# A software pipeline and a flipped operand layout in the tap-generation stage of a long-convolution kernel

## Chip, cores, metric

One core of one Trainium2 chip. The metric is device time of one execution, in microseconds (us), lower is better. The kernel before took 1589.07 us (median of 12 runs, 1585.22 to 1591.90). All profiled runs of known state were fast.

The engines are called PE (TensorE matmuls), PEld (the weight loads of TensorE, which overlap PE), DVE (VectorE), ACT (ScalarE) and POOL (GpSimd), as in the profile.

## The reference, cut to what matters

The program is a state-space long convolution followed by a gated MLP. Only the first part is touched.

```python
def _A_ref(u, A_re, A_im, B_re, B_im, C_re, C_im, log_dt, Dskip):   # L = 2048, D = 576, N = 128
    ...
    P = jnp.exp(logdA[:, :, None] * l[None, None, :])               # (D, N, L)
    K = jnp.einsum('dn,dnl,dn->dl', Cc, P, dB).real                 # the taps, one filter per channel
    ...                                                             # FFT of taps and of u, product, inverse FFT
```

The kernel writes the position as `l = 64*l2 + l1` and splits the power: `K[d, l] = Re sum_n R[n, l1, d] * Q[n, l2, d]`. `R` (64 values of `l1`) is made with exp and sin, `Q` (32 values of `l2`) by repeated doubling (the "Q recurrence"), and the sum over the 128 states is a matmul of PE: 128 x 64 weights from `R`, a 128 x 32 moving operand from `Q`, two (real and imaginary) for each channel. The FFT is a matmul with slabs of cosines and sines.

## The kernel before

The stage works on two interleaved jobs. The first makes the taps, in 36 groups of 16 channels, two groups to a "pair", hence 18 pairs, 64 tap matmuls each. The second transforms the input `u` in 17 blocks of 64 matmuls (the last of 32); each block needs a fresh pair of slabs.

```python
    NCH = 16
    L1VX = Ar.alloc("l1vx", [128, NL1, NCH], BF16)          # 16 channels innermost
    ...
    RR = [Ar.alloc("rr%d" % i, [128, NL1, NCH], BF16) for i in range(2)]
    KST = [Ar.alloc("kst%d" % i, [NL1, NL2, 2 * NCH], BF16, ...) for i in range(2)]

    def r_args(sc):                                         # DVE: arguments of exp and sin
        pa_b = bass.AP(PAB, d0, [pst_of(PAB), [0, NL1], [1, NCH]])
        ...
        dve(lambda e: e.tensor_tensor(ARGA[k][:], L1VX[:], pa_b, ALU.mult), ...)
        dve(lambda e: e.tensor_tensor(ARGP[k][:], L1VX[:], pb_b, ALU.mult), ...)
    def r_acts(scs):                                        # ACT: exp for both groups, then sin
        ...
    def r_products(sc):                                     # DVE: RR = exp*cos, RI = exp*(-sin)
        ...
    def k_matmuls(sc):
        for sl in range(NCH):
            rq = bass.AP(QR, dq, [pst_of(QR), [DH, NL2]])
            lr = bass.AP(RR[c], sl, [pst_of(RR[c]), [NCH, NL1]])   # weights: one element every 32 bytes
            ...
            pe(lambda e: e.matmul(o_ap, lr, rq, start=True, stop=False), ...)
            pe(lambda e: e.matmul(o_ap, li, rqi, start=False, stop=True), ...)
        act(lambda e: e.activation(o_ap, i_ap, ACT.Copy), ...)     # eviction of the taps
        if c == 1:
            st(lambda e: e.dma_start(dst, KST[pr][:]), ...)        # store of the taps

    def gen_slab(dstc, dsts, kc, ks, block_b, nt):
        act(lambda e: e.activation(STMP[0][:, 0:nt, :], PSIS[:, 0:nt, :], ACT.Copy, scale=sphi), ...)
        act(lambda e: e.activation(STMP[1][:, 0:nt, :], PSIC[:, 0:nt, :], ACT.Copy, scale=sphi), ...)
        dve(lambda e: e.scalar_tensor_tensor(out=dstc..., in0=PSIC..., scalar=cphi, in1=STMP[0]...), ...)
        dve(lambda e: e.scalar_tensor_tensor(out=dsts..., in0=PSIS..., scalar=cphi, in1=STMP[1]...), ...)

    def do_pair(pair, nxt):
        ensure_args(pair); r_acts(pair)
        if nxt is not None: ensure_args(nxt)
        for sc in pair: r_products(sc)
        for sc in pair: k_matmuls(sc)
    ...                                                     # first Q recurrence, slabs and blocks mixed in
    for idx, pair in enumerate(pairs0):                     # nine rounds: taps, then a block
        do_pair(pair, nxt)
        slab_step()
        fwd_u_step()                                        # block: 64 matmuls, two evictions on ACT
    ...                                                     # second Q recurrence, slabs and blocks mixed in
    for idx, pair in enumerate(pairs1):                     # nine rounds, no block left
        do_pair(pair, nxt)
        fwd_u_step()
```

After the last round the taps are loaded again from memory in another arrangement (`b_kt<-scr_kd`), and PE transforms them. Everything from there on is the same code in both kernels.

Of the kernel before, what the change touches and what calls it, by code (L numbers as in the profile page):

```python
# [7 lines left out]
ALU = mybir.AluOpType  # L8
# [205 lines left out]
def build_kernel(nc, A_u, A_A_re, A_A_im, A_B_re, A_B_im, A_C_re, A_C_im,  # L214
# [252 lines left out]
    L1VX = Ar.alloc("l1vx", [128, NL1, NCH], BF16)  # L467
# [4 lines left out]
    act(lambda e: e.activation(L1VX[:], bass.AP(L1V, 0, [pst_of(L1V), [1, NL1], [0, NCH]]), ACT.Copy),  # L472
# [4 lines left out]
    ARGA = [Ar.alloc("arga%d" % i, [128, NL1, NCH], BF16) for i in range(NARG)]  # L477
    ARGP = [Ar.alloc("argp%d" % i, [128, NL1, NCH], BF16) for i in range(NARG)]
    ER = ARGA
    CR = [Ar.alloc("cr%d" % i, [128, NL1, NCH], BF16) for i in range(2)]  # L480
    SRN = ARGP
    RR = [Ar.alloc("rr%d" % i, [128, NL1, NCH], BF16) for i in range(2)]
    RI = [Ar.alloc("ri%d" % i, [128, NL1, NCH], BF16) for i in range(2)]
    KST = [Ar.alloc("kst%d" % i, [NL1, NL2, 2 * NCH], BF16, keys=["kst%d_0" % i, "kst%d_1" % i]) for i in range(2)]
    KBANKS = [4, 5, 6, 7]

    def r_args(sc):
        k = sc % NARG
        d0 = sc * NCH
        pa_b = bass.AP(PAB, d0, [pst_of(PAB), [0, NL1], [1, NCH]])  # L490
        pb_b = bass.AP(PBB, d0, [pst_of(PBB), [0, NL1], [1, NCH]])
# [21 lines left out]
    def k_matmuls(sc):  # L513
        c = sc % 2
        pr = (sc // 2) % 2
# [4 lines left out]
        for sl in range(NCH):  # L520
# [4 lines left out]
            lr = bass.AP(RR[c], sl, [pst_of(RR[c]), [NCH, NL1]])  # L525
            li = bass.AP(RI[c], sl, [pst_of(RI[c]), [NCH, NL1]])
# [7 lines left out]
        act(lambda e, o_ap=o_ap, i_ap=i_ap: e.activation(o_ap, i_ap, ACT.Copy),  # L534
            reads=[bkey], writes=["kst%d_%d" % (pr, c)])
        if c == 1:
            dst = bass.AP(Kd, d0 - NCH, [[D, NL1], [NL1 * D, NL2], [1, 2 * NCH]])
            st(lambda e, dst=dst, pr=pr: e.dma_start(dst, KST[pr][:]),
               reads=["kst%d_0" % pr, "kst%d_1" % pr], writes=["kd%d" % (sc // 2)])
# [9 lines left out]
    def gen_slab(dstc, dsts, kc, ks, block_b, nt):  # L549
        cphi = CPHI[:, block_b:block_b + 1]  # L550
        sphi = SPHI[:, block_b:block_b + 1]
        act(lambda e: e.activation(STMP[0][:, 0:nt, :], PSIS[:, 0:nt, :], ACT.Copy, scale=sphi),  # L552
            reads=["psis", "sphi"], writes=["stmp0"])
        act(lambda e: e.activation(STMP[1][:, 0:nt, :], PSIC[:, 0:nt, :], ACT.Copy, scale=sphi),  # L554
            reads=["psic", "sphi"], writes=["stmp1"])
# [27 lines left out]
    def fwd_block(i, srcbuf, srckey, is_k, BK=None, AK=None):  # L583
        r = i % NSLAB
        nyq = (i == NKB - 1)
        groups = [(0, 0), (0, 1)] if nyq else [(0, 0), (0, 1), (1, 0), (1, 1)]
        for (f, h) in groups:
# [15 lines left out]
            if h == 1:  # L603
                np_ = 1 if nyq else 128
                i_ap = bass.AP(PSALL, 2 * f * 512, [[PSPST[0], np_], [512, 2], [1, DH]])
                if not is_k:
# [3 lines left out]
                    act(lambda e, o_ap=o_ap, i_ap=i_ap: e.activation(o_ap, i_ap, ACT.Copy),  # L610
                        reads=[("fps", 2 * f), ("fps", 2 * f + 1)], writes=[dkey])
                else:
# [4 lines left out]
                    act(lambda e, o_ap=o_ap, i_ap=i_ap, sc_ap=sc_ap: e.activation(o_ap, i_ap, ACT.Copy, scale=sc_ap),  # L617
                        reads=[("fps", 2 * f), ("fps", 2 * f + 1), "scol"], writes=[dkey])
# [15 lines left out]

    first_half = list(range(NSC // 2))
    second_half = list(range(NSC // 2, NSC))
    pairs0 = [first_half[i:i + 2] for i in range(0, len(first_half), 2)]
    pairs1 = [second_half[i:i + 2] for i in range(0, len(second_half), 2)]
    fwd_done = [0]
    fwd_loaded = [0]  # L640
    slab_gen = [0]

    def slab_step():
        b = slab_gen[0]
        if b < NKB and b < fwd_done[0] + NSLAB:
            r = b % NSLAB
            gen_slab(SLC[r], SLS[r], "slc%d" % r, "sls%d" % r, b, T)
            slab_gen[0] += 1
# [536 lines left out]
```

## Time and profile before

| stretch of the kernel before (us) | what runs there |
|---|---|
| 62 to 130 | first Q recurrence on DVE, three blocks |
| 130 to 366 | nine rounds of one pair and one block |
| 366 to 434 | second Q recurrence on DVE, the remaining blocks |
| 434 to 578 | nine rounds of one pair alone |
| 578 to 591 | last store of taps and their reload |
| 591 to 1589 | rest of the program, code not touched |

The busy time by stretch of the kernel before comes first. The columns are the stretch with its length, the busy us (and instruction count) of PE, PEld, DVE, ACT and POOL, the granted clock of PE as a share of full speed, the share of the DMA engines and GB/s.

```profile
62.00:130.00 68.00, 28.04 (x192) 20.23 (x192) 56.24 (x59) 23.69 (x25) 0.00 (x0) 0.78 0.00 0
130.00:366.00 236.00, 165.11 (x1166) 136.53 (x1167) 87.97 (x90) 135.87 (x128) 9.84 (x9) 0.69 0.04 6
366.00:434.00 68.00, 37.55 (x276) 27.46 (x273) 56.50 (x59) 23.70 (x24) 0.00 (x0) 0.80 0.00 1
434.00:578.00 144.00, 72.82 (x576) 70.71 (x576) 46.19 (x72) 89.65 (x90) 8.72 (x8) 0.50 0.05 8
```

In the rounds no engine is full: from 130 to 366 us PE is busy 165 of 236 us, ACT 136, DVE 88. A stretch where nobody is full is bound by waits, and the list of waits of 62 to 590 us (engine and line, what it waited for, total us, times, longest) says which:

```profile
PE psall L527 <- DVE b_rr L510: 172.9, 18, 29.4
DVE b_rr L510 <- ACT b_cr L502: 145.5, 36, 12.2
DVE b_slc L556 <- ACT b_stmp L552: 113.8, 17, 9.4
ACT b_kst L534 <- PE psall L529: 105.8, 36, 3.3
```

PE waits for DVE's product, DVE for ACT's cosine, ACT for PE's taps: a circle. The timeline of one round shows it (start, length, engine, line, operation, in brackets the idle time before it and its releaser):

```profile
181.31 1.28 ACT L498 ACT_TABLE_LOAD   x1
182.61 2.00 ACT L498 ACTIVATE b_arga<-b_arga 128x1024 bf16<-128x1024 bf16 x2
...
187.10 0.69 DVE L510 TENSOR_TENSOR b_rr<-b_arga,b_cr 128x1024 bf16<-128x1024 bf16 x1 [7.17 <-ACT b_cr L502]
187.85 0.31 PE L527 MATMUL psall<-b_qr,b_rr 128*64 128x32 bf16 x1 [7.24 <-DVE b_rr L510]
...
196.78 0.59 ACT L534 ACTIVATE b_kst<-psall 64x512 bf16<-64x512 f32 x1 [3.30 <-PE psall L529]
```

ACT begins the exponentials at 181.31 only after it has evicted the block before (copied its result out of `psall`). PE idles 7.24 us until the product at 187.10 frees it, runs taps to 196.7, and then the block from 196.7 to 207.5; in the chain of waits the table load of the next exponentials follows at 208.15, so this round took 26.8 us. Nine rounds with a block take 236 us, nine without 144 us, 16 us each.

The groups of the two matmul operands that the layout touches (line, engine, operation, output<-inputs, shapes, count, busy us and mean ns of one, idle time before):

```profile
L527 PE MATMUL psall<-b_qr,b_rr 128*64 128x32 bf16 x576 | 140.9, 291 | 172.9 <-DVE b_rr L510 172.9
L527 PEld LDWEIGHTS psall<-b_qr,b_rr 128*64 128x64 bf16 x576 | 124.9, 217 | 176.9 <-DVE b_rr L510 176.9
L493 DVE TENSOR_TENSOR b_argp<-b_l1vx,b_pbb 128x1024 bf16<-128x1024 bf16 x36 | 24.7, 686 | 0.0
```

Matmuls overlap, so the 291 ns of one says little about the rate. What counts is the distance from one start to the next: inside a run of taps it is 0.12 us in the timeline, hence 7.7 us for the 64 taps of a pair. In this kernel all runs of taps fall in stretches with a granted clock of 0.50.

The stage ends with the reload of the taps. These lines of the chain of work that ended last (start, length, what) show PE resuming at 590.60 us, right on its landing:

```profile
578.01 3.85 DMA scr_kd<-b_kst
582.37 8.18 DMA b_kt<-scr_kd
590.60 109.44 PE psall L601 x875
```

### The profile page before, as it was taken

The numbers are of one execution on the slowest core, as the hardware profiler recorded it, in microseconds if no ns is written. First come the engines' busy times: TensorE is split into PE (matmuls) and PEld (weight loads), VectorE is DVE, ScalarE is ACT, GpSimd is POOL, SyncE is SP. The second block draws the span as 40 slices with busy tenths as digits, with TensorE's granted clock in tenths as the row PEclk, the third lists the DMA queues.
The fourth block names the chain that finished last, engine by engine and source line by source line (L and its number), as shares of the span: only waits on it lengthen the run. The fifth ranks groups of instructions, "written<-read, shape, count | busy, mean of one in ns | idle before, by whom it ended". The sixth has DMA issues, their size and how long they took to land.

```text
span 1588.8 us, 18520 instructions
## 1 busy us (share of the span) xinstructions
PE 1106.8 (70%) x7945; PEld 808.1 (51%) x7960; DVE 856.7 (54%) x1154; ACT 624.6 (39%) x600; POOL 61.7 (4%) x104
## 2 busy tenths in 40 slices
PE   0344767678255459991799718567866399999997
PEld 0223656566144447771577502122221388888886
DVE  8686343426942325558677607688666733333332
ACT  1524555554266646663254207676555100000000
POOL 0000000000000000000000100000000000000000
PEclk9976676769655559996899859695999699999999
DMA  4100000000000020000001151213432411111100
GB/s 108 41 1 4 4 7 4 7 7 1 1 7 10 8 74 1 1 1 0 22 32 38 74 124 53 70 32 93 113 96 60 138 44 44 44 44 44 44 9 8
DMA packets 92257, 60.15 MB, mean 38 GB/s; under 512 B 51280, under 2 KB 87504, under 8 KB 92176
## 3 DMA queue, kind: packets, MB, share of 16 engines
q1 hardware_dynamic: 86096, 38.52, 9.2%
q0 software_dynamic: 6080, 20.45, 3.9%
q8 instruction: 63, 1.03, 0.3%
q14 instruction: 18, 0.15, 0.0%
HBM read 26.61 MB, written 20.45 MB: 30 GB/s over the span
## 4 chain that ended last, share of the span: by engine, by line
PE 54%; DVE 23%; ACT 16%; DMA 4%; issue 2%; SPq 1%; POOL 0%; ACTq 0%; DVEq 0%; POOLq 0%
PE psall L1100 16%; PE psall L601 14%; PE psall L806 8%; PE psall L529 5%; DVE b_vb L886 4%; PE psall L527 4%; PE psall L1120 4%; ACT b_xsb L881 4%; PE psall L952 2%; DMA b_w2c<-in_B_w_in_dram 2%; ACT b_arga L498 2%; ACT b_x2b L883 2%; DVE b_x2b L885 1%; ACT L502 1%; DVE b_slc L556 1%
## 5 line engine op out<-in xcount | busy, mean ns | idle before, releaser
L1100 PE MATMUL psall<-b_wq,b_z 128*128 128x256 bf16 x2304 | 255.5, 274 | 28.8 <-DVE b_z L1051 28.8
L527 PE MATMUL psall<-b_qr,b_rr 128*64 128x32 bf16 x576 | 140.9, 291 | 172.9 <-DVE b_rr L510 172.9
L1100 PEld LDWEIGHTS psall<-b_wq,b_z 128*128 128x128 bf16 x2304 | 226.3, 98 | 57.1 <-issue 28.7
L556 DVE SCALAR_TENSOR_TENSOR b_slc<-b_psic,b_cphi,b_stmp 128x2048 bf16<-128x2048 bf16 (+1 forms) x50 | 119.0, 2379 | 180.1 <-ACT b_stmp L552 180.1
L527 PEld LDWEIGHTS psall<-b_qr,b_rr 128*64 128x64 bf16 x576 | 124.9, 217 | 176.9 <-DVE b_rr L510 176.9
L952 PE MATMUL psall<-b_w2c,b_hnt 128*128 128x512 bf16 (+3 forms) x393 | 111.6, 410 | 88.5 <-DMA b_w2c<-in_B_w_in_dram 59.6
L601 PE MATMUL psall<-b_xn,b_slc 128*128 128x288 bf16 (+1 forms) x544 | 96.1, 353 | 86.7 <-DVE b_slc L556 67.0
L529 PE MATMUL psall<-b_qi,b_ri 128*64 128x32 bf16 x576 | 140.0, 291 | 13.9 <-DVE b_ri L511 13.9
L806 PE MATMUL psall<-b_t,b_slc 128*128 128x288 bf16 x512 | 129.4, 290 | 27.3 <-DVE b_t L761 27.3
L1106 DVE TENSOR_TENSOR b_gt<-psall,b_bq 128x256 bf16<-128x256 f32 x144 | 61.1, 425 | 145.6 <-PE psall L1100 145.6
L806 PE MATMUL psall<-b_t,b_sls 128*128 128x288 bf16 x512 | 129.0, 289 | 14.7 <-DVE b_t L766 14.7
L552 ACT ACTIVATE b_stmp<-b_psis,b_sphi 128x2048 bf16<-128x2048 bf16 (+1 forms) x50 | 101.4, 2028 | 92.8 <-DVE b_slc L556 92.8
L881 ACT ACTIVATE b_xsb<-psall 128x1024 bf16<-128x1024 f32 (+1 forms) x84 | 75.7, 901 | 155.8 <-PE psall L952 63.3
L529 PEld LDWEIGHTS psall<-b_qi,b_ri 128*64 128x64 bf16 x576 | 124.9, 217 | 16.0 <-DVE b_ri L511 16.0
L886 DVE SCALAR_TENSOR_TENSOR b_vb<-b_x2b,b_xsb 128x1024 bf16<-128x1024 bf16 (+1 forms) x84 | 90.0, 1072 | 77.1 <-ACT b_x2b L883 75.9
L601 PEld LDWEIGHTS psall<-b_xn,b_slc 128*128 128x128 bf16 (+1 forms) x544 | 63.4, 119 | 116.4 <-DVE b_slc L556 66.9
L559 DVE SCALAR_TENSOR_TENSOR b_sls<-b_psis,b_cphi,b_stmp 128x2048 bf16<-128x2048 bf16 (+1 forms) x50 | 119.4, 2389 | 0.0
L952 PEld LDWEIGHTS psall<-b_w2c,b_hnt 128*128 128x128 bf16 (+1 forms) x400 | 35.5, 104 | 164.5 <-issue 129.4
L952 PE MATMUL psall<-b_hnt,b_w1c 128*128 128x512 bf16 (+1 forms) x352 | 95.1, 389 | 29.1 <-ACT b_xsb L881 26.3
L510 DVE TENSOR_TENSOR b_rr<-b_arga,b_cr 128x1024 bf16<-128x1024 bf16 x36 | 24.9, 692 | 145.5 <-ACT b_cr L502 145.5
L554 ACT ACTIVATE b_stmp<-b_psic,b_sphi 128x2048 bf16<-128x2048 bf16 (+1 forms) x50 | 101.4, 2027 | 5.1 <-DVE b_sls L559 5.1
L601 PE MATMUL psall<-b_kt,b_slc 128*128 128x288 bf16 (+1 forms) x544 | 72.6, 293 | 11.5 <-DMA b_kt<-scr_kd 11.5
(147 smaller groups left out, 1456.1 us busy)
## 6 DMA issues: line engine op xcount, KB each, us to landing
scr_wspt<-b_wst POOLq DMA_DIRECT2D x32, 256.0 KB, 2.3
b_wq<-scr_wspt SPq DMA_DIRECT2D x8, 1024.0 KB, 5.9
b_wout<-in_B_w_out_dram SPq DMA_DIRECT2D x1, 2592.0 KB, 9.3
scr_hnd<-b_hn POOLq DMA_DIRECT2D x4, 640.0 KB, 4.5
b_x<-in_A_u_dram SPq DMA_DIRECT2D x4, 576.0 KB, 5.8
scr_rd<-b_tmp POOLq DMA_DIRECT2D x2, 1152.0 KB, 6.5
scr_kd<-b_kst POOLq DMA_DIRECT2D x18, 128.0 KB, 3.8
b_kt<-scr_kd SPq DMA_DIRECT2D x2, 1152.0 KB, 6.9
```

The source lines that it names most:

```text
L527: pe(lambda e, o_ap=o_ap, lr=lr, rq=rq: e.matmul(o_ap, lr, rq, start=True, stop=False), reads=["rr%d" % c, "qr"], writes=([bkey] if sl == ...
L529: pe(lambda e, o_ap=o_ap, li=li, rqi=rqi: e.matmul(o_ap, li, rqi, start=False, stop=True), reads=["ri%d" % c, "qi"], writes=(), publish=(s ...
L552: act(lambda e: e.activation(STMP[0][:, 0:nt, :], PSIS[:, 0:nt, :], ACT.Copy, scale=sphi), reads=["psis", "sphi"], writes=["stmp0"])
L554: act(lambda e: e.activation(STMP[1][:, 0:nt, :], PSIC[:, 0:nt, :], ACT.Copy, scale=sphi), reads=["psic", "sphi"], writes=["stmp1"])
L556: dve(lambda e: e.scalar_tensor_tensor(out=dstc[:, 0:nt, :], in0=PSIC[:, 0:nt, :], scalar=cphi, in1=STMP[0][:, 0:nt, :], op0=ALU.mult, op1 ...
L559: dve(lambda e: e.scalar_tensor_tensor(out=dsts[:, 0:nt, :], in0=PSIS[:, 0:nt, :], scalar=cphi, in1=STMP[1][:, 0:nt, :], op0=ALU.mult, op1 ...
L601: pe(lambda e, o_ap=o_ap, lhsT=lhsT, rhs=rhs, j=j: e.matmul(o_ap, lhsT, rhs, start=(j == 0), stop=(j == T - 1)), reads=[skey, "%s%d" % (sr ...
L806: e.matmul(o_ap, slab[:, i, :], g[:, i, h * DH:(h + 1) * DH], start=first, stop=False),
L881: act(lambda e, xs=xs, ps=gc.ps_ap: e.activation(xs, ps, ACT.Copy), reads=gc.bkeys, writes=["xsb%d" % k])
L886: dve(lambda e, xs=xs, x2=x2, vb=vb: e.scalar_tensor_tensor(out=vb, in0=x2, scalar=GELU_C0, in1=xs, op0=ALU.add, op1=ALU.mult), reads=["xs ...
L952: pe(lambda e, o_ap=o_ap, lhsT=lhsT, rhs=rhs, g=g: e.matmul(o_ap, lhsT, rhs, start=(g == 0), stop=(g == NDT - 1)), reads=[lkeys[g]] + rkey ...
L1100: pe(lambda e, o_ap=o_ap, lhsT=lhsT, rhs=rhs, s_=s_: e.matmul(o_ap, lhsT, rhs, start=(s_ == 0), stop=(s_ == T - 1)), reads=["z2_%d" % s_, ...
```

## The change

Its intent is to break the circle: a block runs on PE while ACT and DVE prepare the next pair, the taps run one round late, their evictions later still, and the 17 blocks are spread over the rounds. Two more edits support this. The slab temporaries move from ACT to DVE for these blocks. And the layout of the `R` operands flips from channel-innermost to position-innermost, so the weights of a tap matmul become contiguous; in exchange, the argument products on DVE get an operand whose innermost step is 0 (one value read 64 times).

```diff
-    L1VX = Ar.alloc("l1vx", [128, NL1, NCH], BF16)
+    L1VX = Ar.alloc("l1vx", [128, NCH, NL1], BF16)
 ...                                     # the same for ARGA, ARGP, CR, RR, RI
+    NKST = 4                            # buffers for evicted taps, 2 before
 ...
-        pa_b = bass.AP(PAB, d0, [pst_of(PAB), [0, NL1], [1, NCH]])
+        pa_b = bass.AP(PAB, d0, [pst_of(PAB), [1, NCH], [0, NL1]])
 ...
-            lr = bass.AP(RR[c], sl, [pst_of(RR[c]), [NCH, NL1]])
+            lr = bass.AP(RR[c], sl * NL1, [pst_of(RR[c]), [1, NL1]])
 ...
+        if dve_only:                    # in gen_slab
+            dve(lambda e: e.tensor_scalar(STMP[0]..., PSIS..., sphi, None, op0=ALU.mult), ...)
+            dve(lambda e: e.tensor_scalar(STMP[1]..., PSIC..., sphi, None, op0=ALU.mult), ...)
 ...                                     # k_matmuls and fwd_block can hand back their evictions (defer=True)
+    while q0:
+        q0.pop(0)()                     # first Q recurrence, now alone
+    gen_fwd(0)
+    for rnd in range(R_TOTAL):
 ...
+        if rnd + 1 < NKB:
+            gen_fwd(rnd + 1)            # slab of the next block (DVE)
+        if cur_pair is not None:
+            ensure_args(cur_pair)
+            r_acts(cur_pair)            # exp and sin of this round's pair (ACT)
+            if pair_idx + 1 < len(pairs_all) and pair_idx + 1 != NP0:
+                ensure_args(pairs_all[pair_idx + 1])
+        if rnd < NKB:
+            pend_fwd_evacs = fwd_block(rnd, XN, "xn", False, evac_eng="act", defer=True)
+        if km_pending is not None:      # taps of the pair of the round before (PE)
+            evs = [k_matmuls(sc, defer=True) for sc in km_pending]
+            pend_k_evacs.append(evs)
+        if cur_pair is not None and pair_idx == NP0 and not q1_done:
+            for grp in qrec_steps(1):
+                grp()                   # second Q recurrence, alone
 ...                                     # older tap evictions, block evictions
+        if cur_pair is not None:
+            for sc in cur_pair:
+                r_products(sc)          # DVE
+            km_pending = cur_pair
```

More of the change, by code (lines that the diff above doesn't have):

```diff
@@ L471, in build_kernel @@
                          allow_small_or_imprecise_dtypes=True), writes=["l1v"])
-    act(lambda e: e.activation(L1VX[:], bass.AP(L1V, 0, [pst_of(L1V), [1, NL1], [0, NCH]]), ACT.Copy),
+    act(lambda e: e.activation(L1VX[:], bass.AP(L1V, 0, [pst_of(L1V), [0, NCH], [1, NL1]]), ACT.Copy),
         reads=["l1v"], writes=["l1vx"])
@@ L476, in build_kernel @@
     Ar.free("pa", "pb")
-    ARGA = [Ar.alloc("arga%d" % i, [128, NL1, NCH], BF16) for i in range(NARG)]
-    ARGP = [Ar.alloc("argp%d" % i, [128, NL1, NCH], BF16) for i in range(NARG)]
+    ARGA = [Ar.alloc("arga%d" % i, [128, NCH, NL1], BF16) for i in range(NARG)]
+    ARGP = [Ar.alloc("argp%d" % i, [128, NCH, NL1], BF16) for i in range(NARG)]
     ER = ARGA
-    CR = [Ar.alloc("cr%d" % i, [128, NL1, NCH], BF16) for i in range(2)]
+    CR = [Ar.alloc("cr%d" % i, [128, NCH, NL1], BF16) for i in range(2)]
     SRN = ARGP
-    RR = [Ar.alloc("rr%d" % i, [128, NL1, NCH], BF16) for i in range(2)]
-    RI = [Ar.alloc("ri%d" % i, [128, NL1, NCH], BF16) for i in range(2)]
-    KST = [Ar.alloc("kst%d" % i, [NL1, NL2, 2 * NCH], BF16, keys=["kst%d_0" % i, "kst%d_1" % i]) for i in range(2)]
+    RR = [Ar.alloc("rr%d" % i, [128, NCH, NL1], BF16) for i in range(2)]
+    RI = [Ar.alloc("ri%d" % i, [128, NCH, NL1], BF16) for i in range(2)]
+    NKST = 4
+    KST = [Ar.alloc("kst%d" % i, [NL1, NL2, 2 * NCH], BF16, keys=["kst%d_0" % i, "kst%d_1" % i]) for i in range(NKST)]
     KBANKS = [4, 5, 6, 7]
@@ L489, in r_args @@
         d0 = sc * NCH
-        pa_b = bass.AP(PAB, d0, [pst_of(PAB), [0, NL1], [1, NCH]])
-        pb_b = bass.AP(PBB, d0, [pst_of(PBB), [0, NL1], [1, NCH]])
+        pa_b = bass.AP(PAB, d0, [pst_of(PAB), [1, NCH], [0, NL1]])
+        pb_b = bass.AP(PBB, d0, [pst_of(PBB), [1, NCH], [0, NL1]])
         dve(lambda e: e.tensor_tensor(ARGA[k][:], L1VX[:], pa_b, ALU.mult), reads=["pab", "l1vx"], writes=["arga%d" % k])
@@ L511, in r_products, with k_matmuls @@
         dve(lambda e: e.tensor_tensor(RI[c][:], ER[k][:], SRN[k][:], ALU.mult), reads=["arga%d" % k, "argp%d" % k], writes=["ri%d" % c])
-    def k_matmuls(sc):
+    def k_matmuls(sc, defer=False):
         c = sc % 2
-        pr = (sc // 2) % 2
+        pr = (sc // 2) % NKST
         d0 = sc * NCH
@@ L524, in k_matmuls @@
             rqi = bass.AP(QI, dq, [pst_of(QI), [DH, NL2]])
-            lr = bass.AP(RR[c], sl, [pst_of(RR[c]), [NCH, NL1]])
-            li = bass.AP(RI[c], sl, [pst_of(RI[c]), [NCH, NL1]])
+            lr = bass.AP(RR[c], sl * NL1, [pst_of(RR[c]), [1, NL1]])
+            li = bass.AP(RI[c], sl * NL1, [pst_of(RI[c]), [1, NL1]])
             pe(lambda e, o_ap=o_ap, lr=lr, rq=rq: e.matmul(o_ap, lr, rq, start=True, stop=False),
@@ L533, in k_matmuls, with evac @@
         i_ap = bass.AP(PSALL, bank * 512, [[PSPST[0], NL1], [1, NL2], [NL2, NCH]])
-        act(lambda e, o_ap=o_ap, i_ap=i_ap: e.activation(o_ap, i_ap, ACT.Copy),
-            reads=[bkey], writes=["kst%d_%d" % (pr, c)])
-        if c == 1:
-            dst = bass.AP(Kd, d0 - NCH, [[D, NL1], [NL1 * D, NL2], [1, 2 * NCH]])
-            st(lambda e, dst=dst, pr=pr: e.dma_start(dst, KST[pr][:]),
-               reads=["kst%d_0" % pr, "kst%d_1" % pr], writes=["kd%d" % (sc // 2)])
+        def evac(o_ap=o_ap, i_ap=i_ap, bkey=bkey, pr=pr, c=c, sc=sc, d0=d0):
+            act(lambda e: e.activation(o_ap, i_ap, ACT.Copy), reads=[bkey], writes=["kst%d_%d" % (pr, c)])
+            if c == 1:
+                dst = bass.AP(Kd, d0 - NCH, [[D, NL1], [NL1 * D, NL2], [1, 2 * NCH]])
+                st(lambda e: e.dma_start(dst, KST[pr][:]),
+                   reads=["kst%d_0" % pr, "kst%d_1" % pr], writes=["kd%d" % (sc // 2)])
+        if defer:
+            return evac
+        evac()
+        return None
     PC = Ar.alloc("pc", [128, NKB, D], BF16, keys=["pc%d" % i for i in range(NKB)])
@@ L547, in build_kernel, with gen_slab @@
     STMP = [Ar.alloc("stmp%d" % r, [128, NKB, 128], BF16) for r in range(2)]
-    def gen_slab(dstc, dsts, kc, ks, block_b, nt):
+    def gen_slab(dstc, dsts, kc, ks, block_b, nt, dve_only=False):
         cphi = CPHI[:, block_b:block_b + 1]
         sphi = SPHI[:, block_b:block_b + 1]
-        act(lambda e: e.activation(STMP[0][:, 0:nt, :], PSIS[:, 0:nt, :], ACT.Copy, scale=sphi),
-            reads=["psis", "sphi"], writes=["stmp0"])
-        act(lambda e: e.activation(STMP[1][:, 0:nt, :], PSIC[:, 0:nt, :], ACT.Copy, scale=sphi),
-            reads=["psic", "sphi"], writes=["stmp1"])
+        if dve_only:
+            dve(lambda e: e.tensor_scalar(STMP[0][:, 0:nt, :], PSIS[:, 0:nt, :], sphi, None, op0=ALU.mult),
+                reads=["psis", "sphi"], writes=["stmp0"])
+            dve(lambda e: e.tensor_scalar(STMP[1][:, 0:nt, :], PSIC[:, 0:nt, :], sphi, None, op0=ALU.mult),
+                reads=["psic", "sphi"], writes=["stmp1"])
+        else:
+            act(lambda e: e.activation(STMP[0][:, 0:nt, :], PSIS[:, 0:nt, :], ACT.Copy, scale=sphi),
+                reads=["psis", "sphi"], writes=["stmp0"])
+            act(lambda e: e.activation(STMP[1][:, 0:nt, :], PSIC[:, 0:nt, :], ACT.Copy, scale=sphi),
+                reads=["psic", "sphi"], writes=["stmp1"])
         dve(lambda e: e.scalar_tensor_tensor(out=dstc[:, 0:nt, :], in0=PSIC[:, 0:nt, :], scalar=cphi,
@@ L581, in make_slab, with fwd_block @@
         store_slab(GENS[r], "gens%d" % r, 1, b, nt)
-    def fwd_block(i, srcbuf, srckey, is_k, BK=None, AK=None):
+    def fwd_block(i, srcbuf, srckey, is_k, BK=None, AK=None, evac_eng="act", defer=False):
         r = i % NSLAB
@@ L586, in fwd_block @@
         groups = [(0, 0), (0, 1)] if nyq else [(0, 0), (0, 1), (1, 0), (1, 1)]
+        evacs = []
         for (f, h) in groups:
@@ L609, in fwd_block @@
                     o_ap = bass.AP(dst, i * D, [[pst_of(dst)[0], np_], [DH, 2], [1, DH]])
-                    act(lambda e, o_ap=o_ap, i_ap=i_ap: e.activation(o_ap, i_ap, ACT.Copy),
-                        reads=[("fps", 2 * f), ("fps", 2 * f + 1)], writes=[dkey])
+                    rk = [("fps", 2 * f), ("fps", 2 * f + 1)]
+                    if evac_eng == "dve":
+                        evacs.append(lambda o_ap=o_ap, i_ap=i_ap, rk=rk, dkey=dkey:
+                                     dve(lambda e: e.tensor_copy(o_ap, i_ap), reads=rk, writes=[dkey]))
+                    else:
+                        evacs.append(lambda o_ap=o_ap, i_ap=i_ap, rk=rk, dkey=dkey:
+                                     act(lambda e: e.activation(o_ap, i_ap, ACT.Copy), reads=rk, writes=[dkey]))
                 else:
@@ L616, in fwd_block @@
                     sc_ap = SCOL[0:np_, i:i + 1]
-                    act(lambda e, o_ap=o_ap, i_ap=i_ap, sc_ap=sc_ap: e.activation(o_ap, i_ap, ACT.Copy, scale=sc_ap),
-                        reads=[("fps", 2 * f), ("fps", 2 * f + 1), "scol"], writes=[dkey])
+                    rk = [("fps", 2 * f), ("fps", 2 * f + 1), "scol"]
+                    evacs.append(lambda o_ap=o_ap, i_ap=i_ap, sc_ap=sc_ap, rk=rk, dkey=dkey:
+                                 act(lambda e: e.activation(o_ap, i_ap, ACT.Copy, scale=sc_ap), reads=rk, writes=[dkey]))
+        if defer:
+            return evacs
+        for ev in evacs:
+            ev()
+        return []
     WH = 1024
@@ L633, in wsp_transpose_step @@
             wsp_si[0] += 1
-    first_half = list(range(NSC // 2))
-    second_half = list(range(NSC // 2, NSC))
-    pairs0 = [first_half[i:i + 2] for i in range(0, len(first_half), 2)]
-    pairs1 = [second_half[i:i + 2] for i in range(0, len(second_half), 2)]
-    fwd_done = [0]
-    fwd_loaded = [0]
-    slab_gen = [0]
-    def slab_step():
-        b = slab_gen[0]
-        if b < NKB and b < fwd_done[0] + NSLAB:
-            r = b % NSLAB
-            gen_slab(SLC[r], SLS[r], "slc%d" % r, "sls%d" % r, b, T)
-            slab_gen[0] += 1
-    def fwd_u_step():
-        if fwd_done[0] < NKB:
-            while slab_gen[0] <= min(fwd_done[0] + 1, NKB - 1):
-                b = slab_gen[0]
-                r = b % NSLAB
-                gen_slab(SLC[r], SLS[r], "slc%d" % r, "sls%d" % r, b, T)
-                slab_gen[0] += 1
-            fwd_block(fwd_done[0], XN, "xn", False)
-            fwd_done[0] += 1
+    pairs_all = [[2 * k, 2 * k + 1] for k in range(NSC // 2)]
+    NP0 = NSC // 4
     argsd = set()
@@ L666, in ensure_args, with gen_fwd @@
                 argsd.add(sc)
-    def do_pair(pair, nxt):
-        ensure_args(pair)
-        r_acts(pair)
-        if nxt is not None:
-            ensure_args(nxt)
-        for sc in pair:
-            r_products(sc)
-        for sc in pair:
-            k_matmuls(sc)
+    def gen_fwd(b):
+        r = b % NSLAB
+        gen_slab(SLC[r], SLS[r], "slc%d" % r, "sls%d" % r, b, T, dve_only=True)
     q0 = qrec_steps(0)
-    slab_step()
-    slab_step()
-    rnd = 0
     while q0:
-        slab_step()
@@ L684, in build_kernel @@
         q0.pop(0)()
-        if rnd % 2 == 1:
-            fwd_u_step()
-        rnd += 1
-    for idx, pair in enumerate(pairs0):
-        nxt = pairs0[idx + 1] if idx + 1 < len(pairs0) else None
-        do_pair(pair, nxt)
-        slab_step()
-        fwd_u_step()
-    q1 = qrec_steps(1)
-    while q1:
-        q1.pop(0)()
-        slab_step()
-        fwd_u_step()
-    for idx, pair in enumerate(pairs1):
-        nxt = pairs1[idx + 1] if idx + 1 < len(pairs1) else None
-        do_pair(pair, nxt)
-        fwd_u_step()
@@ L702, in build_kernel @@
-    while fwd_done[0] < NKB:
-        fwd_u_step()
+    gen_fwd(0)
+    pend_fwd_evacs = []
+    pend_k_evacs = []
+    pair_idx = 0
+    q1_done = False
+    R_TOTAL = max(NKB, len(pairs_all) + 2) + 2
+    km_pending = None
+    for rnd in range(R_TOTAL):
+        for ev in pend_fwd_evacs:
+            ev()
+        pend_fwd_evacs = []
+        if rnd + 1 < NKB:
+            gen_fwd(rnd + 1)
+        cur_pair = pairs_all[pair_idx] if pair_idx < len(pairs_all) else None
+        if cur_pair is not None:
[8 more added lines that the diff above has]
+            pend_k_evacs.append(evs)
+            km_pending = None
+        if cur_pair is not None and pair_idx == NP0 and not q1_done:
+            for grp in qrec_steps(1):
+                grp()
+            q1_done = True
+        if len(pend_k_evacs) > 1:
+            for ev in pend_k_evacs.pop(0):
+                ev()
+        for ev in pend_fwd_evacs:
+            ev()
+        pend_fwd_evacs = []
+        if cur_pair is not None:
+            for sc in cur_pair:
+                r_products(sc)
+            km_pending = cur_pair
+            pair_idx += 1
@@ L705, in build_kernel @@
+    for ev in pend_fwd_evacs:
+        ev()
+    while pend_k_evacs:
+        for ev in pend_k_evacs.pop(0):
+            ev()
+    assert pair_idx == len(pairs_all) and km_pending is None
     if stop_after == "kgen":
@@ L711, in build_kernel @@
     for i in range(2):
-        Ar.free("cr%d" % i, "rr%d" % i, "ri%d" % i, "kst%d" % i)
+        Ar.free("cr%d" % i, "rr%d" % i, "ri%d" % i)
+    for i in range(NKST):
+        Ar.free("kst%d" % i)
     for i in range(NARG):
```

## The prediction

> **What bounds the kernel now.** The change touches only the stretch from about 62 us (first slab) to 590 us (kernel taps reloaded; the chain of waits has the reload landing there, and PE follows without a gap). The rest of the span, about 1000 us, keeps its code. In that stretch no engine is full: the busy table by stretches shows, for 137-230 us, PE 69, DVE 35, ACT 52 of 93 us, and for 440-580 us PE 73, DVE 42, ACT 86 of 140 us. The chain of waits goes round a serial loop: table load, exp, table load, sin on ACT (9.6 us), product on DVE, 64 tap matmul pairs on PE (7.7 us), 64 transform matmuls on PE (9.3-10.7 us), an eviction, and round again. A round with a transform block lasts 25.3-26.8 us, one without 16 us; nine of each, plus two Q recurrences (62-130 and 364-434 us, slabs and blocks mixed in). PE's clock in 440-580 us is 0.50.
>
> **What changes.** (1) Software pipeline: a block runs on PE while ACT and DVE prepare the next pair; tap matmuls run one round late, their evictions two. Transform blocks are spread over 17 of the 18 rounds. (2) Slab temporaries go from ACT (2 x 1.99 us) to DVE; a bf16 scalar op there took 0.88 us at 2304 elements, so about 0.75 each; with the two 2.27 us combinations a slab costs DVE 6.1 us. (3) The layout flip makes one operand of the argument products a value repeated 64 times innermost. [...]+0.54 us x 72 = 39 us of DVE work. (4) Weights of the tap matmuls become contiguous. The pairs run at 0.12 us whatever the clock (1.0 or 0.5), and the isolated 64-column load took 0.195 us against about 0.09 for one column, so I take the stride as their limit. [...]Estimate: pair 0.07 us (two chances in three), else still 0.12.
>
> **New round.** DVE 6.1 + 4.6 + 2.5 = 13.2 us; ACT 11.2; PE 10 + 4.3 = 14.4 (or 10 + 7.7 = 17.8 with unchanged pairs). The waits allow PE to be continuous, so PE sets the round, DVE just behind.
>
> **Sum (end of stretch).** First Q recurrence without slabs ends at 106, first two slabs and arguments at 122-127, round 1 on PE at 129 (nothing gained here: one block done instead of three). Nine rounds x 14.4 to 259. The second Q recurrence is now bare: about 43 us with PE idle except one block, to 303. Pair 9, six rounds less half a block, two last pairs: about 399. Eviction, store and reload 12.4 us as now: 412, against 590.6. That gains 178 us; with 0.12 us pairs 118. Weighted: about 164.
>
> **Prediction: 1425 us, 80% range 1392 to 1478.** Faster by over 2%: 0.96; within: 0.03; slower: 0.01.
>
> **Right or wrong shows in:** argument products about 1.2 us (not 0.69); DVE slab temporaries 0.7-0.8 us; tap pair spacing 0.07 or 0.12; rounds of 14-18 us with PE busy in nearly all of them; one PE gap of about 35 us at the second recurrence; taps reloaded near 412-475 us; everything after unchanged in length.
>
> **What would make it wrong.** Repeated operands staying at 0.69 us (no change if PE bounds); DVE or ACT order blocking PE each round (then 1480-1500); warmer PE clock letting blocks run in 7.85 us, DVE then bounding at 13.4 (1395); later stages changing clock.

The reload lands at 412 us, which gains 178 us with fast taps and 118 us with taps at 0.12 us, weighted about 164, hence 1425 us. The +0.54 us of an argument product (39 us for 72) takes it from 0.69 to 1.225 us. The trace of the kernel before has no product with a repeated value; 1.225 us is the time of another DVE operation on 1024 elements there (`b_vb`, L886). That the product would take as long was not shown beforehand. It enters DVE's round of 13.2 us, which is shorter than PE's 14.4, and in the sum only the arguments before round 1. For the stride as the limit of the taps, the trace before shows the isolated load of 0.195 us for 64 columns against 0.09 for one; that taps keep 0.12 us at both clocks only x1_old_layout shows. The text does not derive the 0.07 us on which the 4.3 us of taps in PE's round rest. By an estimate made afterwards, 0.12 us shortened as the load would be, from 0.195 to 0.09, is 0.055 us, and 0.07 lies between that and no change.

## The result, and the profile after

The changed kernel took 1401.34 us (median of 8 runs, 1400.87 to 1403.40), and its results were correct. The ratio to the kernel before is 0.8820, 95% interval 0.8811 to 0.8828. Ratios here are the mean time of one kernel's fast runs over that of the other's from the same rounds, so they are not quite the ratio of the quoted medians. The kernel before varied by 0.26% between the chips (1588.29 to 1592.42 us), so experiments are compared by these ratios where a few us matter.

The lines of the chain that answer to the reload:

```profile
389.87 3.84 DMA scr_kd<-b_kst
394.23 8.15 DMA b_kt<-scr_kd
402.43 77.68 PE psall L614 x621
```

PE resumes at 402.43 us in place of 590.60: 188.2 us earlier. The span shrank by 188.9 us (1588.8 to 1399.9 in the profiled runs). The rest of the program, 998.2 us before and 997.5 us after, did not move. The whole gain is inside the stage.

Busy time by stretch after, with the columns as before; 128 to 245 are nine rounds, 245 to 298 the second Q recurrence, 298 to 389 the other rounds:

```profile
62.00:128.00 66.00, 9.42 (x65) 6.88 (x66) 60.61 (x70) 13.52 (x20) 0.00 (x0) 0.96 0.00 0
128.00:245.00 117.00, 116.64 (x1152) 93.61 (x1152) 111.30 (x103) 92.81 (x100) 7.66 (x7) 0.89 0.06 9
245.00:298.00 53.00, 14.31 (x128) 10.88 (x128) 47.12 (x61) 19.24 (x28) 1.20 (x2) 0.60 0.02 3
298.00:389.00 91.00, 82.47 (x864) 66.39 (x864) 82.45 (x81) 77.56 (x87) 9.68 (x9) 0.82 0.08 13
```

In the rounds PE is now busy 116.64 of 117 us and DVE 111.30. The circle is gone from the waits of 62 to 402 us:

```profile
PE psall L614 <- ACT b_pc L629: 44.7, 4, 33.1
PE psall L528 <- DVE b_rr L511: 6.7, 2, 4.1
DVE b_rr L511 <- ACT b_cr L503: 4.0, 2, 3.6
```

PE's wait for products fell from 172.9 to 6.7 us and DVE's wait for the cosine from 145.5 to 4.0 us. What remains is 44.7 us of blocks waiting for an eviction: 33.1 us of it is the second Q recurrence, during which ACT's list holds that eviction behind the recurrence's copies.

One round in the timeline after:

```profile
153.41 5.45 PE L614 MATMUL psall<-b_xn,b_slc 128*128 128x288 bf16 x32
153.51 0.69 DVE L511 TENSOR_TENSOR b_rr<-b_arga,b_cr 128x1024 bf16<-128x1024 bf16 x1
155.91 0.75 DVE L559 TENSOR_SCALAR b_stmp<-b_psis,b_sphi 128x2048 bf16<-128x2048 bf16 x1
...
158.69 4.08 PE L614 MATMUL psall<-b_xn,b_sls 128*128 128x288 bf16 x32
161.76 1.23 DVE L493 TENSOR_TENSOR b_arga<-b_l1vx,b_pab 128x1024 bf16<-128x1024 bf16 x1
162.71 0.22 PE L528 MATMUL psall<-b_qr,b_rr 128*64 128x32 bf16 x1
```

PE goes from block to taps to block without idle time, while products, slab and the next arguments run beside it on DVE. And the groups:

```profile
L528 PE MATMUL psall<-b_qr,b_rr 128*64 128x32 bf16 x576 | 67.5, 233 | 11.5 <-DVE b_rr L511 6.7 <-ACT b_kst L537 4.8
L528 PEld LDWEIGHTS psall<-b_qr,b_rr 128*64 128x64 bf16 x576 | 64.7, 130 | 15.6 <-DVE b_rr L511 12.1 <-issue 2.4 <-DVE b_arga L493 0.5
L494 DVE TENSOR_TENSOR b_argp<-b_l1vx,b_pbb 128x1024 bf16<-128x1024 bf16 x36 | 44.1, 1226 | 0.0
```

A weight load fell from 217 to 130 ns, and the distance between tap starts from 0.12 to 0.0565 us, so the 64 taps of a pair take 3.6 us in place of 7.7. An argument product rose from 0.686 to 1.226 us.

One more reading is needed for the experiments: the granted clock around one run of taps after the change. The first line is the tap run, the second the first half of the following block, the third its rest.

```profile
162.80:166.30 3.50, 3.50 (x64) 3.50 (x64) 3.50 (x4) 3.46 (x4) 0.00 (x0) 1.00 0.11 21
166.40:169.70 3.30, 3.30 (x16) 2.09 (x15) 3.30 (x6) 3.24 (x4) 0.00 (x0) 0.51 0.02 5
169.90:176.00 6.10, 6.10 (x51) 4.72 (x49) 6.10 (x5) 4.02 (x6) 1.09 (x1) 1.00 0.08 11
```

PE issued without a pause through the taps (64 matmuls in 3.5 us), yet the clock then fell to half for about 3.4 us. A block that starts so takes 9.62 us; one that does not takes 7.95 us. The blocks in the chain of waits show both: 13.34 us from one to the next (166.50 to 179.84), and 11.67 us (141.80 to 153.47).

The clock fell after seven of the nine runs of taps up to 245 us, not after all. In the clock records of this trace every change lies on a grid of 3.41 us. A dip followed where taps filled at least 81% of one step of this grid (the run from 189.38 to 193.11 us, step from 190.35), and none where they filled at most 76% (138.00 to 141.73, step from 139.15; 202.73 to 206.46). So in these nine rounds it went with when a run of taps fell; why the clock falls the trace doesn't show.

### The profile page after: what moved, and what is told of

Same layout as the page of the kernel before. It is cut to its first block, busy times and chain, and to the rows that moved or that the text cites. A ratio compares the mean times of both kernels' runs of the same rounds, so it can differ in the third digit from the quotient of the medians.

```text
span 1399.9 us, 18558 instructions
## 1 busy us (share of the span) xinstructions
PE 1022.2 (73%) x7945; PEld 730.1 (52%) x7960; DVE 910.9 (65%) x1188; ACT 555.7 (40%) x566; POOL 64.7 (5%) x104
## 4 chain that ended last, share of the span: by engine, by line
PE 55%; DVE 26%; ACT 11%; DMA 4%; issue 2%; SPq 1%; POOL 0%; ACTq 0%; DVEq 0%; POOLq 0%
PE psall L1120 18%; PE psall L614 17%; PE psall L826 9%; DVE b_vb L906 5%; PE psall L1140 5%; ACT b_xsb L901 4%; DMA b_w2c<-in_B_w_in_dram 3%; PE psall L972 2%; ACT b_x2b L903 2%; DVE b_x2b L905 2%; PE psall L528 2%; PE psall L530 2%; DVE b_z1t L920 2%; DVE b_z L920 1%; DVE b_slc L568 1%
## 5 line engine op out<-in xcount | busy, mean ns | idle before, releaser
L614 PE MATMUL psall<-b_xn,b_slc 128*128 128x288 bf16 (+1 forms) x544 | 93.3, 346 | 153.8 <-DVE b_slc L568 109.0
L826 PE MATMUL psall<-b_t,b_sls 128*128 128x288 bf16 x512 | 128.7, 289 | 14.7 <-DVE b_t L786 14.7
L564 ACT ACTIVATE b_stmp<-b_psis,b_sphi 128x2048 bf16<-128x2048 bf16 (+1 forms) x33 | 67.6, 2048 | 92.2 <-DVE b_slc L568 92.2
L914 ACT ACTIVATE b_sgb<-b_vb 128x1024 bf16<-128x1024 bf16 (+1 forms) x84 | 78.3, 932 | 1.3 <-DVE b_vb L906 1.3
L972 PEld LDWEIGHTS psall<-b_hnt,b_w1c 128*128 128x128 bf16 (+1 forms) x360 | 29.4, 96 | 93.5 <-issue 74.6
L528 PE MATMUL psall<-b_qr,b_rr 128*64 128x32 bf16 x576 | 67.5, 233 | 11.5 <-DVE b_rr L511 6.7
L826 PEld LDWEIGHTS psall<-b_t,b_slc 128*128 128x128 bf16 x512 | 50.5, 99 | 44.4 <-DVE b_t L781 27.6
L528 PEld LDWEIGHTS psall<-b_qr,b_rr 128*64 128x64 bf16 x576 | 64.7, 130 | 15.6 <-DVE b_rr L511 12.1
L1140 PE MATMUL psall<-b_wout,b_z1t 128*128 128x288 bf16 x576 | 71.9, 286 | 0.0
```

The costliest lines, as they stand in the source:

```text
L528: pe(lambda e, o_ap=o_ap, lr=lr, rq=rq: e.matmul(o_ap, lr, rq, start=True, stop=False), reads=["rr%d" % c, "qr"], writes=([bkey] if sl == ...
L614: pe(lambda e, o_ap=o_ap, lhsT=lhsT, rhs=rhs, j=j: e.matmul(o_ap, lhsT, rhs, start=(j == 0), stop=(j == T - 1)), reads=[skey, "%s%d" % (sr ...
L826: e.matmul(o_ap, slab[:, i, :], g[:, i, h * DH:(h + 1) * DH], start=first, stop=False),
L914: act(lambda e, vb=vb, sg=sg: e.activation(sg, vb, ACT.Sigmoid, scale=GELU_S), reads=["vb%d" % k], writes=["sgb%d" % k])
L972: pe(lambda e, o_ap=o_ap, lhsT=lhsT, rhs=rhs, g=g: e.matmul(o_ap, lhsT, rhs, start=(g == 0), stop=(g == NDT - 1)), reads=[lkeys[g]] + rkey ...
L1140: pe(lambda e, o_ap=o_ap, lhsT=lhsT, rhs=rhs, ft=ft: e.matmul(o_ap, lhsT, rhs, start=(ft == 0), stop=(ft == NFT - 1)), reads=["z1t_%d" % f ...
```

## The experiments

Four questions: how much is the schedule and how much the layout; did moving the slab temporaries matter; what bounds the round now, PE or DVE; and what would help further.

A round's length below is the mean distance between starts of the slab combination on DVE in the timeline (lines `b_slc`), from the second one after 120 us on, up to the last but one before the second Q recurrence (the last of these rounds prepares no arguments for a next pair, so that DVE has less to do).

| kernel | time us | ratio to before | round us | argument product us | tap to tap us |
|---|---|---|---|---|---|
| changed | 1401.34 | 0.8820 | 12.9 | 1.226 | 0.0565 |
| x1_old_layout | 1463.06 | 0.9212 | 17.3 | 0.682 | 0.12 |
| x2_layout_alone | 1525.84 | 0.9608 | - | 1.217 | 0.057 |
| x3_slab_temps_act | 1419.13 | 0.8937 | 14.8 | 1.217 | 0.0565 |
| x4_group4 | 1399.42 | 0.8808 | 13.6 | 0.682 | 0.061 |
| x4_group2 (one run) | 1395.63 | - | 13.0 | 0.682 | 0.0565 |
| x4_group8 (one run) | 1465.30 | - | 17.3 | 0.682 | 0.12 |
| x5_interleave_k1 | 1436.39 | 0.9036 | 14.7 | 1.216 | 0.055 |
| x5_interleave_k4 | 1439.45 | 0.9060 | 15.4 | 0.683 | 0.061 |
| x7_split2_k1 | 1402.02 | 0.8808 | 12.8 | 1.216 | 0.0565 |
| x7_split2_k2 | 1389.25 | 0.8728 | 11.9 | 0.682 | 0.0565 |
| x7_split4_k2 | 1395.92 | 0.8770 | 12.3 | 0.682 | 0.0565 |
| x6_two_kst | 1406.18 | 0.8834 | 13.0 | - | 0.0565 |

### 1. The new schedule with the old layout

```diff
-    L1VX = Ar.alloc("l1vx", [128, NCH, NL1], BF16)      # and ARGA, ARGP, CR, RR, RI
+    L1VX = Ar.alloc("l1vx", [128, NL1, NCH], BF16)
-            lr = bass.AP(RR[c], sl * NL1, [pst_of(RR[c]), [1, NL1]])
+            lr = bass.AP(RR[c], sl, [pst_of(RR[c]), [NCH, NL1]])
```

> The new schedule with the old layout (tap index outer, channel inner). Theory (two parts: overlap, and shorter weight loads): argument products back at 0.69 us, tap matmuls back at 0.12 us each, so the tap phase of a round is 7.7 us in place of 3.6 and PE alone sets the round at about 17.5 us (block 9.5-10.5); 17 such rounds cost about 75 us, so about 1475 us. Rival (the overlap did it all, since the tap matmuls are hidden behind the Vector and Scalar work): at most 1410 us.

Measured: 1463.06 us (1461.43 to 1464.73), ratio 0.9212, interval 0.9198 to 0.9226. Taps are again 0.12 us apart, PE is busy all 100 us from 128 to 228, a round takes 17.3 us. The time is 12 us under the expected 1475, and far above the 1410 of the rival. The schedule alone, with the slab temporaries on DVE and the four buffers that come with it here, is worth 125 us (1588.29 on that chip).

### 2. The new layout with the old schedule

```diff
-    L1VX = Ar.alloc("l1vx", [128, NL1, NCH], BF16)      # and the others; argument and weight views too
+    L1VX = Ar.alloc("l1vx", [128, NCH, NL1], BF16)
```

> The old schedule with the new layout. Theory: each of the 18 serial rounds loses 64 x 0.064 = 4.1 us of tap matmuls, about 74 us, and the dearer argument products (1.22 us) are mostly off the chain, costing 2 to 5 us at the two starts: about 1518 us. Rival (layout pays only together with the overlap): 1580 us or more.

Measured: 1525.84 us (1525.43 to 1526.57), ratio 0.9608, interval 0.9593 to 0.9622. That is 8 us above the expected 1518, and far below the 1580 of the rival. The layout alone is worth 62 us, although it adds 38 us of DVE work (72 products, 0.531 us longer each). In the serial loop of the kernel before, the taps were on the path and the arguments mostly were not. The two parts add up: 125 + 62 is 187, and together they gave 188. So the gain is split about two to one between schedule and layout, and neither needs the other.

### 3. Slab temporaries back on ACT

```diff
-        gen_slab(SLC[r], SLS[r], "slc%d" % r, "sls%d" % r, b, T, dve_only=True)
+        gen_slab(SLC[r], SLS[r], "slc%d" % r, "sls%d" % r, b, T)
```

> The changed kernel with the slab temporaries of the 17 input blocks back on ACT (2 x 1.99 us a round). Theory: ACT goes from 11.2 to 15.0 us a round and becomes the longest of the three; rounds of about 15 us instead of 13, so about 1401 + 17 x 1.9 = 1433 us. Rival (PE sets the round at 13.2 us and ACT has room enough): within 8 us of 1401.

Measured: 1419.13 us (1418.73 to 1420.58), ratio 0.8937, interval 0.8924 to 0.8950. That is 18 us slower than the changed kernel, about half of the expected loss. The direction was right, as this line of the busy table (128 to 250 us) shows: ACT is busy 119.24 of 122 us, PE no longer is.

```profile
128.00:250.00 122.00, 111.89 (x1054) 87.79 (x1052) 93.68 (x79) 119.24 (x112) 7.66 (x7) 0.85 0.05 9
```

A round is 14.8 us against 12.9, and 17 of those would cost 32 us. The traces show why not all of it arrived. From the first block of the nine rounds to the end of their taps the loss is 15 us (131.6 against 116.7), and from the first block after the second Q recurrence to the last (298.16 to 363.86 us in the changed kernel) it is 8 us (74.1 against 65.7). But the first of the nine blocks started 2.7 us sooner (125.26), and the second Q recurrence and the end were about 2 us shorter.

### 4. Is DVE the bound? Two, four or eight channels innermost

If `G` channels stand innermost, the argument product reads a short run of `G` values again and again in place of one value, and the weights of a tap matmul are `2*G` bytes apart.

```diff
+    KG = 4                              # 2, 4 or 8
-        pa_b = bass.AP(PAB, d0, [pst_of(PAB), [1, NCH], [0, NL1]])
+        pa_b = bass.AP(PAB, d0, [pst_of(PAB), [KG, NCH // KG], [0, NL1], [1, KG]])
-            lr = bass.AP(RR[c], sl * NL1, [pst_of(RR[c]), [1, NL1]])
+            lr = bass.AP(RR[c], sl // KG * NL1 * KG + sl % KG, [pst_of(RR[c]), [KG, NL1]])
```

> The changed kernel with 4 channels innermost: weights of one channel 8 bytes apart, argument operand repeated in groups of 4 adjacent values. [...]tap matmuls stay at 0.0565 us; if any stride above one element is slow, they go to 0.08-0.12 us and the time to 1430-1475 us. The argument products should be back at 0.69 us, the DVE round at 10.6 us instead of 12.8. If PE sets the rounds nearly as much as DVE does, the gain is small, about 10 us (1390 us); if DVE alone sets them, PE would fall to warm blocks of 7.9 us and rounds near 11.5 us: about 1375 us.

Measured: 1399.42 us (1398.16 to 1401.01), ratio 0.8808, interval 0.8794 to 0.8823, not separable from the changed kernel. The product is back at 0.682 us and DVE has 20 us of slack in 100, but the round is 13.6 us:

```profile
128.00:228.00 100.00, 100.00 (x929) 79.47 (x928) 79.20 (x86) 84.34 (x92) 6.56 (x6) 0.87 0.06 9
```

PE is busy all 100 us. The taps are a little slower (0.061 us apart), and the blocks of the nine rounds, 9.69 us for the first and 9.62 for the others, are as long as one that started at half clock in the changed kernel (9.62); the granted clock is 0.87 on average. An estimate of the reason: four steps of the 3.41 us grid in the changed kernel's clock records are 13.65 us, nearly a round here, so every run of taps would fall on such a grid in the same way. So DVE alone was not what held the changed kernel, but with PE slower at the same time this run does not isolate it.

> 2 channels innermost: weights 4 bytes apart[...] 0.0565 to 0.062 us a tap matmul. Argument products: a repeated pair of adjacent values; 0.69 us if pairs are enough[...], 1.22 us if not. About 1399 us.

Measured: 1395.63 us in a single run (state unknown; before was 1589.87 on that chip). Product 0.682 us, taps 0.0565 us apart: both good at once. The round did not get shorter (13.0 us against 12.9), with PE busy all 100 of 100 us from 128 to 228 and DVE only 80. The 6.6 us that it gained (by the ratio of its one run to before) came outside the full rounds: the first block starts at 126.29 in place of 127.95, and the second Q recurrence and the last rounds, where DVE is on the path, end 6.5 us earlier in all (reload landed at 395.95 in place of 402.43).

> 8 channels innermost: weights of one channel 16 bytes apart[...] tap matmuls at 0.12 us each as with 32 bytes apart, and about 1463 us. If the cost grows with the stride: between 0.062 and 0.12, about 1425 us.

Measured: 1465.30 us in a single run (state unknown). Taps are 0.12 us apart again, a weight load takes 217 ns. Together with the other layouts this gives the distance between taps against the step between weights: 0.0565 us at 2 and 4 bytes, 0.061 at 8, 0.12 at 16, 0.12 at 32. Going from 8 to 16 bytes doubles it, and beyond that nothing changes. At 8 bytes taps were 8% slower than contiguous ones. Why the step lies between 8 and 16 bytes the runs don't show.

### 5. Taps in runs of four between the block's matmuls

The theory was that the half clock after a run of taps (0.51 in the changed kernel) could be avoided by mixing the taps into the block.

```diff
+    TAPG = 4
+                if queue and j % TAPG == TAPG - 1:       # in the loop over a block's matmuls
+                    for _ in range(TAPG // 2):
+                        if queue: queue.pop(0)()         # one real and one imaginary tap matmul
```

> The changed kernel (layout as changed) with its tap matmuls spread among the block matmuls, 4 of one after 4 of the other, in place of one run of 64. Theory (the run of 3.6 us of small tap matmuls lets the granted clock fall, so every block begins slow and takes 9.6 us in place of 7.9): the granted clock in the rounds goes from 0.89 to about 1.0 and the PE part of a round from 13.2 to about 11.5 us; but DVE needs 12.8 us a round, so only 0.4 us a round is gained: about 1395 us. Rival (the slow start belongs to something else, such as the wait for the slab): clock and time unchanged, 1401 us.

> The same interleaving with 4 channels innermost (argument products at 0.69 us, tap matmuls at 0.062). Theory (PE by its clock and DVE by its argument products are two bounds of almost the same height, so each relief alone gains nothing): rounds go to about 12 us, limited by PE at full clock, and 15 of them gain about 1.6 us each: about 1373 us. Rival: 1395 us or more, as with either relief alone.

Measured: 1436.39 us (1434.83 to 1438.21), ratio 0.9036, with the changed layout, and 1439.45 us (1437.33 to 1442.27), ratio 0.9060, with four channels innermost. Both are far slower than expected, by 41 and 66 us. The clock part was right: 0.95 and 0.98 in 128 to 228 us. But the timeline of the second kernel (PE only) shows what mixing costs:

```profile
160.35 0.23 PE L536 MATMUL psall<-b_qi,b_ri 128*64 128x32 bf16 x1
160.41 0.23 PE L534 MATMUL psall<-b_qr,b_rr 128*64 128x32 bf16 x1
160.47 0.23 PE L536 MATMUL psall<-b_qi,b_ri 128*64 128x32 bf16 x1
160.64 0.66 PE L626 MATMUL psall<-b_xn,b_slc 128*128 128x288 bf16 x4
161.23 0.25 PE L534 MATMUL psall<-b_qr,b_rr 128*64 128x32 bf16 x1
```

A cycle lasts 0.96 us (160.27 to 161.23 for the first tap of each). Four block matmuls at 0.1225 us (their distance at a granted clock of 1.00: in the kernel before, 32 of this size took 3.92 us, 611.31 to 615.23) and four taps at 0.061 us make 0.73 us. About 0.23 us is lost in each cycle, sixteen times a round, 3.6 us: more than the 1.67 us that a half-clock start costs.

### 6. Fewer switches: two runs of 32, four runs of 16

The same queue, filled in longer runs, with either layout. This is a two-by-two test: relieve DVE alone (two channels innermost, above), relieve PE's clock alone (two runs, changed layout), or both.

```diff
+    TAPG = 32                           # 16 for four runs
+                nb[0] += 1              # block matmuls issued so far
+                if queue and nb[0] % TAPG == 0:
+                    for _ in range(TAPG // 2):
+                        if queue: queue.pop(0)()
```

> The same two runs of 32 taps with the layout of the changed kernel (argument products at 1.22 us). Theory: TensorE could do the round in about 11.9 us, but VectorE needs 12.8 us and is then alone the bound: VectorE fully busy in the rounds, TensorE not, 1390 to 1400 us, a gain of 10 us at the most. Rival (TensorE alone is the bound of the changed kernel): as fast as the version with two channels innermost, about 1378 us.

Measured: 1402.02 us (1400.85 to 1402.70), ratio 0.8808, interval 0.8795 to 0.8821: no gain that can be separated. The clock is up (0.96) and PE waits now and then; DVE is nearly full, and the round is 12.8 us, DVE's own sum:

```profile
128.00:228.00 100.00, 98.68 (x1013) 79.08 (x1014) 97.37 (x92) 88.32 (x96) 7.68 (x7) 0.96 0.07 11
```

> Two channels innermost (argument products at about 0.68 us, taps still 0.0565 us apart) and the 64 tap matmuls of a round in two runs of 32, one in the middle of the block matmuls and one at their end. Theory: after the change VectorE (12.8 us) and TensorE (cold blocks of 9.6 us plus taps of 3.6 us) bound the round together, and relieving one alone gains next to nothing; here both are relieved: tap runs of about 1.8 us should not cool the clock, blocks take 7.85 us, two switches of 0.22 us, a round of about 11.9 us, VectorE about 10 us: about 1378 us. Rival (the switches cost more than the cold clock, as with the runs of four): 1395 us or more.

Measured: 1389.25 us (1388.53 to 1389.64), ratio 0.8728, interval 0.8715 to 0.8741, the fastest. The clock is 0.98, with taps in runs of 1.8 us (32 at 0.0565), and the round 11.9 us, as expected to a tenth of a microsecond; the time is 11 us above the 1378 expected.

```profile
128.00:228.00 100.00, 100.00 (x1053) 81.24 (x1052) 84.88 (x93) 87.32 (x95) 7.68 (x7) 0.98 0.07 11
```

By ratio, against a before of 1590 us, clock alone gave 2 us, DVE alone about 7 (one run, none of it in the full rounds), both 15. In the full rounds neither alone shortened anything that matters (12.8 us with the clock relieved, 13.0 with DVE relieved, against 12.9), and both together took them to 11.9. That is what two bounds at the same height look like.

The missing 11 us are a matter of counting. The expectation does not give its sum, but a gain of 23 us is what 1.4 us (13.3 to 11.9) in each of 16 rounds make. In fact the mean round before the edit was 12.9, not 13.3, and about 13 rounds are of this kind: 13 us, and with the first block starting 1.6 us earlier (126.38) that is the 15 us measured. The last two pairs run after the last block, and there neither PE nor DVE is the bound, as the chain of this kernel shows between the last block matmuls and the store:

```profile
345.57 4.04 PE psall L627 x32
...
360.78 1.28 ACT L503
362.07 2.00 ACT b_arga L503 x2
364.10 1.28 ACT L507
...
375.21 3.86 DMA scr_kd<-b_kst
```

Of these 25 us (349.6 to 374.8) about 17 are table loads, exponentials and sines of ACT, which the edit does not touch; the rest is evictions and the taps of the last pair.

> As the first of these, with four runs of 16 taps. If each switch between the two kinds of matmul costs about 0.22 us, a round costs 0.4 us more than with two runs, 12.3 us, about 1383 us. If the loss of the runs of four came from something else than the number of switches, it is as fast as with two runs or far slower.

Measured: 1395.92 us (1394.91 to 1396.78), ratio 0.8770, interval 0.8757 to 0.8783. The round is 12.3 us as expected, and the time is again 13 us above, for the same reason. The price of a switch now rests on five kernels. Take the distance of one cycle from the timelines and subtract the block matmuls (0.1225 us each) and the taps (0.0565 us each, 0.061 with four channels innermost):

| kernel | cycle us | matmuls and taps us | rest us |
|---|---|---|---|
| interleaved, changed layout (4 + 4) | 0.92 | 0.72 | 0.20 |
| interleaved, four channels innermost (4 + 4) | 0.96 | 0.73 | 0.23 |
| four runs (16 + 16) | 3.075 | 2.86 | 0.21 |
| two runs (32 + 32) | 5.945 | 5.73 | 0.22 |
| changed kernel, full-clock round (64 + 64) | 11.67 | 11.46 | 0.21 |

The rest is the same whatever the length of the runs: a fixed 0.2 us for going from block to taps and back. What in PE causes it the runs don't show.

### 7. Two buffers for evicted taps in place of four

```diff
-    NKST = 4
+    NKST = 2
```

> The changed kernel with two buffers for evicted taps in place of four. A store of taps lands about 3.9 us after its issue and a buffer is used again two rounds, about 26 us, later: nothing waits for it, 1401 us within 3 us. Rival (the two more buffers are part of the gain): slower than 1406 us, with ScalarE waiting for stores.

Measured: 1406.18 us (1405.83 to 1406.76), ratio 0.8834, interval 0.8819 to 0.8849, overlapping that of the changed kernel (0.8811 to 0.8828). On its chip the kernel before took 1592.42 us; scaled to 1589.07 it is 1403.2. In the rounds no eviction waits for a store. One does at the very end, 3.6 us, where the last pairs come closer together than 26 us, and the reload lands at 405.80 in place of 402.43. So by the traces the extra buffers are worth about 3 us, all of it at the end; the times alone do not separate it. The expectation overlooked the end, and its rival was wrong about the rounds.

## Why the prediction was right

**The bound before: right.** The serial loop is gone from the list of waits (172.9 to 6.7 us, 145.5 to 4.0 us), and putting in the schedule alone gave 125 us.

**Where the gain lies: right.** Predicted gain 178 us with fast taps, ending in a reload at 412 us; the reload landed at 402.43, and the rest of the program kept its length within 1 us. The time, 1401.34, lies inside the range of 1392 to 1478. The point, 1425, was 24 us too high. Of these, 14 us come from having weighted the two cases of the tap spacing, and the other 10 us are sizes. That it was only 10 is in part luck, since errors in the sum offset each other. The nine rounds took 116.7 us (127.95 to 244.64), not 130. From the end of the second Q recurrence to the last store it took 98.4 us (291.5 to 389.87), where 96 were forecast, although six rounds there should have saved nearly 10 us more at 12.8 us in place of 14.4. So about 12 us were left out of that part of the sum; PE's wait for products and a slab before the block at 298.16 is in them.

**Argument products: right.** Predicted 0.69 to 1.22 us; measured 0.686 to 1.226. That a value read 64 times would take so long was an estimate; this run shows it, and x4_group2 that a pair of values read again and again is enough to get the old 0.682 us.

**Tap spacing: right in direction, too timid in size.** The estimate was 0.07 us with two chances in three; 0.0565 was measured. Over 64 taps that is 3.6 us, not 4.3 or so. One reason that the prediction gives for the stride as the limit, the same 0.12 us at both clocks, is not in the trace of the kernel before, where all taps ran at 0.50; x1_old_layout shows it. The predicted fallback, 0.12 us, is what the strided layouts measured, and the forecast for it came true as well: a gain of 118 us, and 125 measured.

**PE's round: right about who bounds it in the first nine rounds, 1.5 us too long.** The forecast was PE 14.4, DVE 13.2 "just behind". Measured: PE 13.34 with a half-clock start and 11.67 without, 12.9 on average; DVE 12.8. That PE came out ahead of DVE is a matter of 0.1 us, and in the rounds after the second Q recurrence DVE sets the pace (five starts of the slab combination in a row 12.80 us after the one before, from 295.17 to 359.15), and PE waits now and then. The mis-sized terms are the taps (3.6 in place of 4.3) and the block: 10 us was read from the blocks of the kernel before (10.27 and 10.72 us in the chain), where PE had idled before the taps; in the pipeline, after a first one of 10.05, the blocks up to 245 us took 7.95 to 9.62, and with the old layout 9.2 to 10.0. The warning that a warmer clock would leave DVE as the bound did not come true in the nine rounds: two blocks of the first eight took 7.95 us, but PE stayed full around them. It describes the kernel with two runs of taps and the changed layout.

**The second Q recurrence: right.** Forecast bare, about 43 us, to 303. It ran alone from 248.7 to 291.5 us, 42.8 us, and the next block started at 298.16. It came earlier since nine rounds were shorter. The one long wait of PE was 33.1 us; about 35 was forecast.

**Slab temporaries: right.** 0.753 us on DVE; leaving them on ACT would have cost 18 us.

**Not foreseen:** that PE's clock drops to half after most runs of taps (seven of nine up to 245 us) although PE is busy all through them (3.50 of 3.50 us in the one shown), and that PE and DVE end so close that relieving only one gives next to nothing.

## What to carry to other kernels

When no engine is full, follow the waits until they close into a circle, and let each engine work on another round's data; the gain can be summed beforehand from the durations in the trace. Once the pipeline stands, two engines may bind at the same height: a test that relieves one alone shows nothing, so test both reliefs together before calling either useless. And check how weights lie in memory: a step of 4 bytes between them cost nothing here (0.0565 us from one of these small matmuls to the next, as at 2 bytes), 8 little (0.061), and 16 and 32 doubled the distance (0.12).
